# One output product in 93 places is split into two 64-row halves and issued between the halves of three U/V products

## The chip, the cores and the metric

The kernel runs on one core of one Trainium2 chip. The metric is the device time of one execution in microseconds (us). The engines named below are PE (TensorE, the matrix engine; PEld is its weight loads), DVE (VectorE), ACT (ScalarE), POOL (GpSimd) and SP (SyncE, which issues the DMAs). Each engine takes its instructions in program order.

## The reference, cut to what matters

```python
# attention through 49 agents: q, k, v are (4, 12544, 128), agents (4, 49, 128)
agent_v = softmax(scale * agents @ k.T) @ v          # per batch, 49 x 128
x = softmax(scale * q @ agents.T) @ agent_v          # per batch, 12544 x 128
x = x.reshape(50176, 128)
# feed-forward with a maximum of three: w1, w2, w3 are 128 x 768, w_out 768 x 128
h = maximum(maximum(x @ w1, x @ w2), x @ w3)
out = h @ w_out
```

## The kernel before, in words

**What is computed where.** Each batch first folds agent_v with the weights into a table G with 49 rows, stored twice, at partitions 0 to 48 and 64 to 112. Its columns hold agent_v times (w3-w1) (768 columns), times (w2-w1) (768), and a linear part through w1 and w_out. The maximum of three is taken as w1 + max(relu(w3-w1), w2-w1), where the w1 part goes through the linear table. For the fifth hidden block (f = 4) the second difference is added onto the relu in place and a second relu follows; there the columns are w3-w2 and w2-w1.

**Stages.** The 50176 rows of q are worked on in 49 stages, s = 0 to 48. Stage s has 1024 rows, or 8 tiles of 128 rows; the exponentials of its scores, e.s (128 x 512), hold the odd tiles' 49 agents at partitions 64 to 112 and the even tiles' at 0 to 48. Six hidden blocks f of 128 columns are computed in each stage. The operations on the path of the change, with their names in the order string and their lines in the kernel before, are these:

- u.s.f and v.s.f (PE, L558): one U or V product. It is a pair of matmuls of 49 rows each, one on the upper and one on the lower half of the array's rows, each with 512 columns. They write the two banks of one PSUM buffer of class UV. There are 3 UV buffers.
- a.s.f (ACT, L571, or L565 for f = 4): relu of u.s.f. For f other than 4 it writes a bf16 tile and so frees the UV buffer; for f = 4 it writes in place, and v.s.4 accumulates onto it.
- x.s.f (DVE, L574: maximum of v.s.f with the relu; or ACT, L568 for f = 4): writes r.s.f, the hidden block in bf16, and frees the UV buffer.
- li.s.o (PE, L582) and p.s.o.f (PE, L592): for each half o of the stage's tiles, an output tile o.s.o (128 x 512, PSUM class OM, 2 buffers) takes the linear part and then six output products. One output product p.s.o.f is four matmuls of 128 rows by 128 columns, with r.s.f as the weights and w_out as the moving operand.
- ov.s.o (DVE, L599): scales the output tile by the reciprocals of the softmax sums, once all six p.s.o.f are in.

Beside these run sc and ex (scores and exponentials), su and re (softmax sums and their reciprocals on DVE, L550), qt and qe (transposes of q, evacuated by DVE, L527), the work on k and v of the next batch (ks, kv on PE, kx on ACT, va on DVE, L465), casts on POOL, and loads and stores on SP.

**Array tilings.** The class Plan marks three kinds of PE work: ROW (two halves of the array's rows work beside each other: u and v), FULL (the whole array: p, li, su, ks, kv, transposes) and COL (two halves of its columns: sc).

**What sets the order.** The order of all operations is written out by hand in the string ORDER, one word an operation; the number behind a slash is the buffer that its new tile takes. Emit.run walks through the words, makes the new tiles and issues the operation. A new tile in a buffer makes its first writer wait until the last reader of the buffer's former tile is done. Since each engine runs its own words in order, ORDER fixes five queues.

Of the kernel before, what the change touches and what calls it, by code (L numbers as in the profile page):

```python
# [611 lines left out]
def kernel(  # L612
# [17 lines left out]
    plan = Plan()  # L630
    graph(plan, em)
    order, given = [], {}
    for word in ORDER.split():
        name, _, slots = word.partition("/")
        order.append(name)
        if slots:
            given[name] = [int(x) for x in slots.split(",")]
# [22 lines left out]
p.0.1.0 u.2.3/0 ov.0.1 u.2.4/2 a.2.3/2 v.1.0/1 ks1.1/1 x.1.0/4 li.1.0/0 p.1.0.2 a.2.4 su.2 p.1.0.3 p.1.0.5 re.2/0 v.2.5/0 kx1.1/0  # L660
u.2.1/1 v.2.4 x.2.5/6 a.2.1/0 p.1.0.4 kv1.1 p.1.0.1 p.1.0.0 x.2.4/3 va1.1 v.2.1/0 ov.1.0/1 v.2.3/1 vc1.2/0 sc.3/1 x.2.3/1 u.2.2/2
ex.3/0 li.1.1/0 p.1.1.4 kc1.3/1 a.2.2/1 p.1.1.2 x.2.1/0 ks1.2/1 p.1.1.0 v.2.2/1 kx1.2/3 kc1.4/2 u.2.0/2 kt1.3/0 p.1.1.5 x.2.2/4
a.2.0/2 kv1.2 su.3 p.1.1.1 p.1.1.3 kl1.5/11 u.3.5/0 re.3/2 va1.2 v.2.0/1 ov.1.1 vl1.5/5 a.3.5/1 u.3.1/2 li.2.0/1 ql.6/3 x.2.0/7
p.2.0.3 p.2.0.4 kl1.6/6 a.3.1/0 qt.4/0 ql.7/10 u.3.4/0 qe.4/0 kt1.4/2 u.3.3/1 a.3.4 v.3.5/2 p.2.0.5 x.3.5/2 p.2.0.2 p.2.0.0
a.3.3/2 vc1.3/0 p.2.0.1 kl2.1/12 sc.4/0 ov.2.0/2 v.3.4 ex.4/1 v.3.3/2 ea1.0/0 v.3.1/1 x.3.4/5 x.3.3/8 li.2.1/1 vl2.0/7 p.2.1.5
ks1.3/0 su.4 p.2.1.4 kx1.3/1 x.3.1/6 u.3.2/0 u.4.5/2 a.3.2/2 kv1.3 p.2.1.3 kc1.5/1 p.2.1.0 va1.3 re.4/1 v.3.2/1 a.4.5/0 u.3.0/0
x.3.2/7 li.3.0/0 qc.5/0 p.3.0.5 kt1.5/0 a.3.0/1 p.2.1.2 p.2.1.1 u.4.3/2 ov.2.1 ea1.1 v.3.0/1 a.4.3/2 u.4.4/0 vl1.7/9 x.3.0/0
p.3.0.3 ql.9/11 qt.5/1 vc1.5/0 a.4.4 p.3.0.4 u.4.1/2 qe.5/0 v.4.5/1 qc.6/0 a.4.1/1 v.4.4 x.4.5/4 p.3.0.2 p.3.0.1 x.4.4/1 p.3.0.0
ea1.2 sc.5/1 ov.3.0/3 v.4.1/1 u.4.2/2 ex.5/2 kc1.6/0 v.4.3/0 x.4.1/3 li.3.1/0 a.4.2/0 p.3.1.4 p.3.1.5 vc1.4/2 ks1.4/1 kt1.6/1
x.4.3/5 u.5.5/1 kx1.4/3 v.4.2/2 p.3.1.0 a.5.5/1 qc.7/1 su.5 kv1.4 x.4.2/0 kl1.7/2 u.4.0/0 vl1.6/6 p.3.1.2 a.4.0/2 p.3.1.1 kc1.8/2  # L670
kl1.9/10 p.3.1.3 re.5/0 va1.4 u.5.3/2 ov.3.1 v.4.0/1 a.5.3/0 u.5.4/0 ql.8/3 x.4.0/8 qt.6/1 li.4.0/0 a.5.4 p.4.0.3 u.5.1/2 qe.6/0
v.5.5/1 a.5.1/2 vl1.8/8 p.4.0.5 x.5.5/6 p.4.0.0 p.4.0.1 sc.6/1 v.5.1/2 ex.6/0 v.5.4 u.5.2/1 x.5.1/7 ql.10/5 p.4.0.2 a.5.2/1
p.4.0.4 li.4.1/1 p.4.1.5 ov.4.0/4 v.5.2/2 x.5.4/2 qc.9/0 vl2.3/4 u.6.5/1 x.5.2/4 p.4.1.4 ks1.5/0 a.6.5/2 p.4.1.3 vc1.7/2 p.4.1.0
v.5.3/0 u.6.4/2 kx1.5/0 kl1.10/0 u.5.0/1 x.5.3/8 a.6.4 p.4.1.1 kv1.5 su.6 p.4.1.2 a.5.0/1 re.6/2 va1.5 v.5.0/0 ov.4.1 v.6.4
ql.14/11 qt.7/0 x.6.4/0 x.5.0/3 li.5.0/1 p.5.0.5 p.5.0.3 u.6.3/1 vc1.6/0 vl1.10/9 v.6.5/2 qe.7/0 a.6.3/1 u.6.1/0 p.5.0.1 x.6.5/5
# [6 lines left out]
u.8.5/1 st.1 va1.7 u.8.4/2 ov.6.1 a.8.5/1 v.7.0/0 li.7.0/1 x.7.0/5 p.7.0.3 p.7.0.1 a.8.4 qt.9/0 ql.13/8 u.8.1/1 qe.9/0 v.8.5/0
a.8.1/2 v.8.4 x.8.5/4 p.7.0.5 p.7.0.2 vl2.1/6 p.7.0.0 x.8.4/2 p.7.0.4 sc.9/0 ov.7.0/0 v.8.3/0 ex.9/0 v.8.1/1 u.8.2/2 x.8.3/1
ks1.8/1 a.8.2/1 li.7.1/0 su.9 p.7.1.4 p.7.1.2 x.8.1/9 p.7.1.3 kx1.8/3 kc2.0/2 u.9.5/2 v.8.2/0 a.9.5/0 p.7.1.0 re.9/2 x.8.2/6
u.8.0/1 kv1.8 vc1.9/2 a.8.0/2 p.7.1.1 p.7.1.5 va1.8 u.9.3/2 ov.7.1 v.8.0/0 ea1.6 a.9.3/1 u.9.4/1 x.8.0/8 qt.10/1 li.8.0/0 a.9.4
ea1.7 p.8.0.2 p.8.0.5 qe.10/0 u.9.1/2 v.9.5/0 kc1.10/1 a.9.1/2 v.9.4 x.9.5/0 p.8.0.4 p.8.0.0 p.8.0.1 qc.14/2 x.9.4/5 kt1.10/0
p.8.0.3 sc.10/1 ov.8.0/1 v.9.1/0 ex.10/1 u.9.2/2 kc2.1/0 v.9.3/1 x.9.1/3 kl2.5/11 a.9.2/0 ks1.9/0 li.8.1/1 st.2 p.8.1.3 vc2.3/3
p.8.1.0 st.5 kx1.9/0 x.9.3/7 u.9.0/2 kt2.0/2 v.9.2/0 a.9.0/2 su.10 p.8.1.5 qc.11/0 p.8.1.1 x.9.2/8 kv1.9 p.8.1.2 ql.12/4 p.8.1.4
ea1.8 u.10.5/2 ql.15/9 v.9.0/1 re.10/1 va1.9 a.10.5/0 u.10.3/0 ql.18/12 ov.8.1 qc.13/1 qt.11/0 kl2.4/0 x.9.0/2 li.9.0/1 a.10.3/1
# [174 lines left out]
```

## Time and profile before

| what | value |
|---|---|
| median of 2 runs | 449.47 us (448.12 to 450.82) |
| the profiled execution, device time | 448.96 us |
| its span, first to last instruction | 447.1 us |
| granted TensorE clock, mean | 0.988 |
| PE, DVE, ACT, POOL busy | 421.8, 392.1, 393.6, 169.5 us |
| matmuls, and weight loads | 5260 each |

How to read it: a busy time is the time in which at least one instruction of the engine was under way. Matmuls overlap in the pipeline and their ends are modelled, so a busy PE may still have short gaps between streams. PEld overlaps PE. An idle time is put down to whatever released the engine, and gaps of 0.15 us or less are not listed as waits. Everything between the stages runs beside everything else, so a share of the span says little until one asks what waits for what.

### The profile page before, as it was taken

Reading aid. Unit: us, or ns where it says so; the run is one execution under the profiler, and the core shown is the slowest. Engines: PE = TensorE matmul, PEld = TensorE weight load, DVE = VectorE, ACT = ScalarE, POOL = GpSimd, SP = SyncE. Lnnn points to the kernel's source line nnn. Section 1 sums busy time; section 2 is a strip of 40 time slices with the busy share of each in tenths; the row PEclk is TensorE's granted clock in tenths of the full one; section 3 lists DMA queues with packets and bytes.
Section 4 is the critical chain, followed back from the end, with each engine's and each line's share of the span. In section 5 each row is a group of like instructions: output and inputs, shape, how many; then the busy total and the mean of one; then the engine's idle time right before and its main releaser. Section 6 shows DMA issues by size and latency. Waiting matters only on the chain.

```text
span 447.1 us, 12853 instructions
## 1 busy us (share of the span) xinstructions
PE 421.8 (94%) x5260; PEld 270.8 (61%) x5260; DVE 392.1 (88%) x496; ACT 393.6 (88%) x461; POOL 169.5 (38%) x176
## 2 busy tenths in 40 slices
...
DMA packets 97045, 121.98 MB, mean 273 GB/s; under 512 B 70423, under 2 KB 73179, under 8 KB 96987
## 3 DMA queue, kind: packets, MB, share of 16 engines
...
q10 hardware_dynamic: 203, 0.10, 0.1%
...
## 4 chain that ended last, share of the span: by engine, by line
PE 83%; DMA 8%; DVE 3%; issue 2%; POOL 2%; ACT 1%; SPq 1%; DVEq 0%; POOLq 0%
PE UV L558 35%; PE OM L592 31%; PE OM L582 6%; DMA LD<-in_v_dram 4%; PE OM L533 3%; DVE R L574 2%; PE OM L523 2%; DMA LD<-in_k_dram 2%; PE OM L376 2%; PE OM L359 2%; DMA LD<-in_q_dram 1%; PE OM L545 1%; SPq L325 1%; DVE OS L599 1%; POOL QB L517 1%
## 5 line engine op out<-in xcount | busy, mean ns | idle before, releaser
L574 DVE TENSOR_TENSOR R<-UV,AS 128x1024 bf16<-128x1024 f32 x245 | 293.4, 1219 | 17.8 <-PE UV L558 12.9
L571 ACT ACTIVATE AS<-UV 128x1024 bf16<-128x1024 f32 x245 | 246.3, 1024 | 17.8 <-PE UV L558 13.5
L558 PE MATMUL UV<-EQ,G 49*128 49x512 bf16 (+1 forms) x1248 | 181.7, 371 | 0.9
L592 PE MATMUL OM<-wo_bf,R 128*128 128x128 bf16 x2352 | 180.4, 220 | 0.0
L592 PEld LDWEIGHTS <-R 128*128 128x128 bf16 x2352 | 139.8, 98 | 43.4 <-issue 41.1
L558 PEld LDWEIGHTS <-G 49*128 49x128 bf16 x1248 | 61.5, 94 | 61.8 <-issue 21.7
L517 POOL CAST QB<-LD 128x1024 bf16<-128x1024 f32 x49 | 51.1, 1048 | 98.4 <-DMA LD<-in_q_dram 50.3
L335 POOL CAST KB<-LD 128x1152 bf16<-128x1152 f32 (+2 forms) x45 | 49.7, 1116 | 60.4 <-DMA LD<-in_k_dram 42.8
L599 DVE TENSOR_TENSOR OS<-OM,RC 128x512 f32<-128x512 f32 x98 | 67.1, 684 | 3.6 <-PE OM L592 2.5
L335 POOL CAST VB<-LD 128x1152 bf16<-128x1152 f32 (+1 forms) x33 | 37.3, 1137 | 47.7 <-DMA LD<-in_v_dram 14.7
L565 ACT ACTIVATE UV<-UV 128x1024 f32<-128x1024 f32 x49 | 49.8, 1017 | 2.5 <-PE UV L558 1.2
L568 ACT ACTIVATE R<-UV 128x1024 bf16<-128x1024 f32 x49 | 50.1, 1023 | 1.7 <-PE UV L558 1.2
L582 PE MATMUL OM<-G,EQ 128*128 128x256 bf16 x196 | 37.9, 276 | 0.0
L539 ACT ACTIVATE EQ<-OM 128x512 bf16<-128x512 f32 x49 | 29.5, 602 | 0.9 <-PE OM L533 0.6
L474 POOL TENSOR_TENSOR EA<-EA,EK 128x441 f32<-128x441 f32 x27 | 27.6, 1023 | 4.8 <-ACT EK L365 4.1
L347 DVE COPY KT<-UV 128x1152 bf16<-128x1152 bf16 (+1 forms) x12 | 8.2, 700 | 17.3 <-PE UV L342 17.3
L582 PEld LDWEIGHTS <-EQ 128*128 128x128 bf16 x196 | 12.6, 97 | 15.6 <-issue 14.2
L533 PE MATMUL OM<-QT,agT 128*64 128x512 bf16 (+1 forms) x104 | 20.4, 398 | 0.2 <-DMA QT<-QB 0.2
L365 ACT ACTIVATE EK<-OM 128x441 bf16<-128x441 f32 (+1 forms) x33 | 17.8, 540 | 2.9 <-POOL EA L474 1.6
L376 PE MATMUL OM<-EK,VB 128*128 128x49 bf16 x392 | 17.3, 186 | 2.7 <-ACT VB L333 1.4
L359 PEld LDWEIGHTS <-KT 128*128 128x128 bf16 x392 | 14.6, 98 | 7.5 <-issue 4.5
L376 PEld LDWEIGHTS <-VB 128*128 128x128 bf16 x392 | 14.3, 97 | 7.9 <-issue 5.0
...
## 6 DMA issues: line engine op xcount, KB each, us to landing
...
KT<-KB SPq DMA_TRANSPOSE x33, 7.0
```

What stands on the lines that cost most here:

```text
L335: (self.nc.gpsimd if eng == POOL else self.nc.vector).tensor_copy(out=out, in_=src)
L376: self.nc.tensor.matmul(out, vb[:, j, :], e[:, j * A:(j + 1) * A], start=False, stop=True, skip_group_check=True)
L517: return lambda: self.nc.gpsimd.tensor_copy(out=self.t[f"qb.{s}"], in_=self.t[f"q.{s}"][:, :GT, :])
L533: self.nc.tensor.matmul(self.t[f"qs.{s}"][h * H:(h + 1) * H, jj * P:(jj + pairs) * P], self.agT[:, b, :], self.t[f"qT.{s}"][:, 2 * jj + h: ...
L558: self.nc.tensor.matmul(t[:, h, jj * P:(jj + pairs) * P], self.t[f"G{b}"][h * H:h * H + A, c + f * P:c + (f + 1) * P], self.t[f"e.{s}"][h ...
L565: return lambda: self.nc.scalar.activation(self.t[f"u.{s}.{f}"], self.t[f"u.{s}.{f}"], AF.Relu)
L568: return lambda: self.nc.scalar.activation(self.t[f"r.{s}.{f}"], self.t[f"u.{s}.{f}"], AF.Relu)
L571: return lambda: self.nc.scalar.activation(self.t[f"a.{s}.{f}"], self.t[f"u.{s}.{f}"], AF.Relu)
L574: return lambda: self.nc.vector.tensor_tensor(out=self.t[f"r.{s}.{f}"], in0=self.t[f"v.{s}.{f}"], in1=self.t[f"a.{s}.{f}"], op=ALU.max)
L582: self.nc.tensor.matmul(self.t[f"o.{s}.{o}"][:, i * 2 * C:(i + 1) * 2 * C], self.t[f"e.{s}"][:, jj * P:(jj + 1) * P], self.t[f"G{of[jj]}"] ...
L592: self.nc.tensor.matmul(self.t[f"o.{s}.{o}"][:, c:c + C], self.t[f"r.{s}.{f}"][:, h, jj * P:(jj + 1) * P], self.wo_bf[:, f, :], start=Fals ...
L599: self.nc.vector.tensor_tensor(out=self.t[f"os.{s}"][:, j:j + 4, :], in0=self.t[f"o.{s}.{o}"].rearrange("p (j c) -> p j c", c=C), in1=self ...
```

## The change

In 93 places, four words of ORDER become one word joined by plus signs: three U/V products and one output product. Emit.run hands such a word to the new function beside. It splits the output product's 128 contraction rows in two halves of 64, so that four matmuls become eight, and issues one half of them behind the first half of the first U/V product and the other half behind the last U/V product. Behind the first half stands a further matmul of one column (named fence), into the buffer that the third U/V product is going to use. Which half of the rows comes first alternates for each output tile. Buffer numbers are those of before. On ACT, DVE, POOL and SP the order of the operations is the same as before; on PE 295 of 1536 places in the order hold another operation.

```diff
-    def run(self, plan, order, given):
+    def run(self, plan, order, given, joint):
         self.place = plan.places(order, given)
+        done = set(x for k, v in joint.items() for x in v if x != k)
         for name in order:
-            o = plan.ops[plan.index[name]]
-            for t in o["new"]:
+            if name in done:
+                continue
+            group = joint.get(name, [name])
+            if len(group) > 1:
+                self.beside(plan, group[:-1], group[-1])
+                continue
+            for t in plan.ops[plan.index[name]]["new"]:
                 self.new(plan.tiles[t], t)
-            o["fn"]()
+            plan.ops[plan.index[name]]["fn"]()
+
+    def beside(self, plan, hidden, product):
+
+        ps, o, pf = (int(x) for x in product.split(".")[1:])
+
+        def one(name, h):
+            kind, s, f = name.split(".")
+            s, f = int(s), int(f)
+            start = kind == "u" or f != FI
+            t = self.t[f"u.{s}.{f}" if kind == "u" or not start else f"v.{s}.{f}"]
+            c = (C31 if kind == "u" else C21) + f * P
+            return self.nc.tensor.matmul(t[:, h, :], self.t[f"G{s // WHOLE}"][h * H:h * H + A, c:c + P], self.t[f"e.{s}"][h * H:h * H + A, :],
+                                  start=start, stop=True, skip_group_check=True)
+
+        def rows(k):
+            for i in range(4):
+                h, jj = i % 2, 2 * o + i // 2
+                self.nc.tensor.matmul(self.t[f"o.{ps}.{o}"][:, i * C:(i + 1) * C],
+                                             self.t[f"r.{ps}.{pf}"][k:k + H, h, jj * P:(jj + 1) * P], self.wo_bf[k:k + H, pf, :],
+                                             start=False, stop=True, skip_group_check=True)
+
+        for t in plan.ops[plan.index[hidden[0]]]["new"] + plan.ops[plan.index[hidden[1]]]["new"]:
+            self.new(plan.tiles[t], t)
+        a = self.side.get((ps, o), 1)
+        self.side[ps, o] = 1 - a
+        one(hidden[0], 1 - a)
+        rows(a * H)
+        fence = self.new("UV", plan.ops[plan.index[hidden[2]]]["use"][0])
+        self.nc.tensor.matmul(fence[:, 0, :1], self.wo_bf[a * H:a * H + H, pf, :], self.wo_bf[a * H:a * H + H, pf, :1], start=True, stop=True,
+                              skip_group_check=True)
+        one(hidden[0], a)
+        one(hidden[1], 1 - a)
+        for t in plan.ops[plan.index[hidden[2]]]["new"]:
+            self.new(plan.tiles[t], t)
+        one(hidden[1], a)
+        one(hidden[2], 1 - a)
+        one(hidden[2], a)
+        rows((1 - a) * H)
...
-p.0.0.5 kt1.2/0 x.0.2/6 ks1.0/1 p.0.0.0 u.1.2/2 kx1.0/1 v.1.3/0 vc1.0/0 a.1.2/0 kl1.3/5 p.0.0.4 x.1.3/7 u.2.5/1 vl1.2/3 p.0.0.2
+p.0.0.5 kt1.2/0 x.0.2/6 ks1.0/1 p.0.0.0 kx1.0/1 vc1.0/0 kl1.3/5 u.1.2/2+v.1.3/0+u.2.5/1+p.0.0.4 a.1.2/0 x.1.3/7 vl1.2/3 p.0.0.2
...
+ov.31.1 a.33.3/2 vc3.10/2 qt.34/0 x.32.0/9 li.32.0/1 a.33.4 p.32.0.5 qc.37/0 qe.34/1 u.33.1/0+v.33.4+v.33.5/2+p.32.0.3 a.33.1/1
...
```

In 67 of the places the output product stood directly ahead of the three U/V products on PE before, in 18 it stood between them, and in 8 directly behind them. Where one of the three is a v.s.4, which accumulates onto an old tile, it never stands third; in 26 places it stands second.

More of the change, by code (lines that the diff above doesn't have):

```diff
@@ L632 @@
     order, given = [], {}
+    joint = {}
     for word in ORDER.split():
[L634 to L637, printed above, removed]
+        names = []
+        for part in word.split("+"):
+            name, _, slots = part.partition("/")
+            names.append(name)
+            if slots:
+                given[name] = [int(x) for x in slots.split(",")]
+        order += names
+        if len(names) > 1:
+            joint[names[0]] = names
     assert sorted(order) == sorted(plan.index)
     with tc.manual_schedule():
-        em.run(plan, order, given)
+        em.side = {}
+        em.run(plan, order, given, joint)
 ORDER = """
@@ L660 @@
[L660 to L675, printed above, removed]
+kl1.8/8 vc1.1/0 a.1.4 qe.3/0 qc.4/0 u.1.0/2+v.1.4+v.1.1/0+p.0.1.4 a.1.0/0 x.1.1/2 p.0.1.1 vl1.3/4 p.0.1.5 p.0.1.3 x.1.4/0 p.0.1.2
@@ new lines @@
+u.2.3/0+u.2.4/2+v.1.0/1+p.0.1.0 ov.0.1 a.2.3/2 ks1.1/1 x.1.0/4 li.1.0/0 p.1.0.2 a.2.4 su.2 p.1.0.3 re.2/0 kx1.1/0
+v.2.5/0+v.2.4+u.2.1/1+p.1.0.5 x.2.5/6 a.2.1/0 p.1.0.4 kv1.1 p.1.0.1 p.1.0.0 x.2.4/3 va1.1 v.2.1/0 ov.1.0/1 v.2.3/1 vc1.2/0 sc.3/1
+x.2.3/1 u.2.2/2 ex.3/0 li.1.1/0 p.1.1.4 kc1.3/1 a.2.2/1 p.1.1.2 x.2.1/0 ks1.2/1 p.1.1.0 v.2.2/1 kx1.2/3 kc1.4/2 u.2.0/2 kt1.3/0
+p.1.1.5 x.2.2/4 a.2.0/2 kv1.2 su.3 p.1.1.1 kl1.5/11 re.3/2 va1.2 vl1.5/5 u.3.5/0+v.2.0/1+u.3.1/2+p.1.1.3 ov.1.1 a.3.5/1 li.2.0/1
@@ L682 @@
[L682 to L689, printed above, removed]
@@ new lines @@
+v.7.2/1 a.7.0/2 p.6.1.3 x.7.2/3 p.6.1.4 ql.11/9 ks1.7/1 v.7.1/2 kx1.7/0 u.8.3/0 x.7.1/0 p.6.1.1 a.8.3/0 kv1.7 su.8 p.6.1.0 re.8/0
+st.1 va1.7 u.8.5/1+u.8.4/2+v.7.0/0+p.6.1.5 ov.6.1 a.8.5/1 li.7.0/1 x.7.0/5 p.7.0.3 p.7.0.1 a.8.4 qt.9/0 ql.13/8 qe.9/0
+u.8.1/1+v.8.4+v.8.5/0+p.7.0.5 a.8.1/2 x.8.5/4 p.7.0.2 vl2.1/6 p.7.0.0 x.8.4/2 p.7.0.4 sc.9/0 ov.7.0/0 v.8.3/0 ex.9/0 v.8.1/1
+u.8.2/2 x.8.3/1 ks1.8/1 a.8.2/1 li.7.1/0 su.9 p.7.1.4 p.7.1.2 x.8.1/9 p.7.1.3 kx1.8/3 kc2.0/2 re.9/2
+u.9.5/2+v.8.2/0+u.8.0/1+p.7.1.0 a.9.5/0 x.8.2/6 kv1.8 vc1.9/2 a.8.0/2 p.7.1.1 va1.8 ea1.6 u.9.3/2+v.8.0/0+u.9.4/1+p.7.1.5 ov.7.1
@@ new lines @@
+a.12.5/2 li.11.0/0 u.12.3/1+v.11.0/2+u.12.4/0+p.11.0.4 a.12.3/1 st.3 x.11.0/9 p.11.0.5 p.10.1.5 p.10.1.4 a.12.4 ov.10.1 st.4
+u.12.1/1+v.12.4+v.12.5/2+p.11.0.1 a.12.1/0 x.12.5/4 p.11.0.3 p.11.0.0 p.11.0.2 x.12.4/6 sc.13/1 ov.11.0/7 v.12.1/1 v.12.3/2
+ex.13/1 kt2.4/2 u.12.2/0 x.12.1/3 li.11.1/0 a.12.2/2 p.11.1.5 ks2.1/1 su.13 p.11.1.2 x.12.3/5 kx2.1/3 ql.17/0 v.12.2/1 u.12.0/0
+kv2.1 a.12.0/0 p.11.1.4 x.12.2/2 u.13.3/2 p.11.1.3 a.13.3/1 p.11.1.0 re.13/1 va2.1 u.13.5/1+u.13.4/0+v.12.0/2+p.11.1.1 ov.11.1
@@ new lines @@
+qc.21/2 x.19.5/3 kt2.9/0 p.18.0.0 p.18.0.4 p.18.0.5 x.19.4/5 p.18.0.1 kc2.10/2 sc.20/0 ov.18.0/1 qd.21/2 v.19.1/2 ex.20/2 v.19.3/1
+u.19.2/0 x.19.1/0 ea2.5 li.18.1/1 a.19.2/0 p.18.1.4 ks2.8/0 ql.24/5 p.18.1.1 x.19.3/6 st.14 u.20.5/2 kx2.8/0 v.19.2/0 vl3.5/4
+a.20.5/1 p.18.1.2 kv2.8 st.13 x.19.2/1 u.19.0/1 kt2.10/1 p.18.1.5 a.19.0/2 p.18.1.3 va2.8 kl3.2/8
+u.20.3/2+v.19.0/0+u.20.4/1+p.18.1.0 ov.18.1 a.20.3/0 x.19.0/7 su.20 li.19.0/1 p.19.0.2 kc3.0/1 st.9 p.19.0.3 a.20.4 re.20/2
+vc3.1/0 u.20.1/2+v.20.4+v.20.5/0+p.19.0.1 a.20.1/2 x.20.5/4 p.19.0.5 kt3.0/2 p.19.0.4 p.19.0.0 x.20.4/9 vc2.10/2 sc.21/0 ov.19.0/6
@@ new lines @@
+v.21.3/1 kc3.2/2 vl3.4/10 ex.22/1 v.21.1/0 u.21.2/2 x.21.3/3 ks2.10/0 a.21.2/1 li.20.1/1 fo2/0 p.20.1.2 vl3.6/11 p.20.1.5 x.21.1/1
+v.21.2/1 kx2.10/2 u.22.5/2 p.20.1.1 a.22.5/0 kv2.10 x.21.2/5 u.21.0/0 kl3.3/8 to2 a.21.0/2 su.22 va2.10 re.22/1 nr2/0,2
+u.22.3/2+v.21.0/1+u.22.4/0+p.20.1.0 a.22.3/1 x.21.0/7 st.16 p.20.1.4 li.21.0/0 p.21.0.2 a.22.4 p.20.1.3 ov.20.1
+u.22.1/1+v.22.4+v.22.5/2+p.21.0.3 a.22.1/2 x.22.5/8 p.21.0.0 kc3.4/1 st.15 p.21.0.5 p.21.0.1 x.22.4/9 p.21.0.4 sc.23/1 ov.21.0/5
+qc.24/2 v.22.1/2 kt3.1/1 ex.23/2 u.22.2/1 v.22.3/0 x.22.1/4 a.22.2/0 li.21.1/0 vc3.0/2 p.21.1.4 p.21.1.2 vl3.3/5 p.21.1.5 x.22.3/0
@@ new lines @@
+x.27.2/9 u.28.5/1 a.27.0/2 p.26.1.5 li.27.0/0 p.27.0.4 ov.26.1 v.27.0/2 a.28.5/0 u.28.4/0 x.27.0/0 p.27.0.3 p.27.0.5 a.28.4
+v.28.5/1 sc.29/1 x.28.5/6 u.28.1/2 ex.29/2 p.27.0.2 p.27.0.1 a.28.1/2 p.27.0.0 v.28.4 ov.27.0/6 v.28.1/1 x.28.4/7 li.27.1/1
+x.28.1/1 p.27.1.2 ks3.5/0 kx3.5/3 v.28.3/2+u.28.2/0+u.29.5/1+p.27.1.5 x.28.3/5 a.28.2/2 p.27.1.4 kc3.6/2 kv3.5 p.27.1.0 su.29
+a.29.5/0 v.28.2/0 re.29/0 va3.5 u.28.0/2 kc3.8/1 kt3.6/0 x.28.2/0 li.28.0/0 a.28.0/1 p.27.1.3 p.28.0.3 ea3.3 vl3.9/1
+u.29.3/1+v.28.0/0+u.29.4/2+p.27.1.1 ov.27.1 a.29.3/2 x.28.0/2 qc.32/0 a.29.4 p.28.0.2 qt.30/1 qe.30/0
@@ new lines @@
+u.29.1/1+v.29.4+v.29.5/0+p.28.0.4 a.29.1/1 x.29.5/3 p.28.0.0 p.28.0.5 p.28.0.1 ov.28.0/2 x.29.4/8 sc.30/1 ex.30/0 v.29.1/0
+x.29.1/9 ql.38/4 v.29.3/1 x.29.3/4 u.29.2/2 a.29.2/0 li.28.1/0 p.28.1.0 ks3.6/1 p.28.1.1 su.30 kx3.6/2 u.30.5/0 a.30.5/1 v.29.2/2
+p.28.1.5 kl3.10/9 kc3.7/2 ql.39/8 kt3.7/1 re.30/1 x.29.2/6 p.28.1.2 vc3.7/3 u.29.0/1 a.29.0/2 p.28.1.3 kv3.6 va3.6
+u.30.4/0+v.29.0/2+u.30.3/1+p.28.1.4 ov.28.1 a.30.4 a.30.3/0 x.29.0/7 ql.33/10 qd.32/0 ql.34/5 qc.33/2 qc.34/0 kt3.8/0 st.26
+li.29.0/1 p.29.0.1 p.29.0.5 v.30.4 x.30.4/5 sc.31/0 ql.37/7 v.30.5/2 x.30.5/0 u.30.1/1 a.30.1/2 p.29.0.4 p.29.0.0 p.29.0.3 ex.31/1
@@ new lines @@
+v.30.1/0+u.30.2/2+v.30.3/1+p.29.0.2 ov.29.0/0 x.30.1/1 a.30.2/1 x.30.3/2 li.29.1/1 ks3.7/0 kx3.7/1 p.29.1.2 p.29.1.4 st.21 st.24
+qd.33/1 kt3.9/1 p.29.1.0 u.31.5/0 a.31.5/2 v.30.2/2 x.30.2/7 p.29.1.3 p.29.1.1 u.30.0/1 a.30.0/0 p.29.1.5 kv3.7 ov.29.1 su.31
+re.31/2 u.31.3/0 a.31.3/1 vc3.8/3 vl3.10/10 v.30.0/2 u.31.4/1 a.31.4 x.30.0/3 li.30.0/1 p.30.0.4 p.30.0.5 va3.7 ea3.4 ea3.5
+u.31.1/0+v.31.4+v.31.5/2+p.30.0.1 a.31.1/0 x.31.5/9 x.31.4/4 p.30.0.3 p.30.0.0 p.30.0.2 ov.30.0/3 sc.32/0 ex.32/2 v.31.3/2
@@ new lines @@
+u.31.2/0 v.31.1/1 x.31.3/8 ks3.8/1 a.31.2/2 li.30.1/0 ql.35/0 p.30.1.1 vc3.9/2 p.30.1.3 x.31.1/6 ql.43/5 v.31.2/2 kx3.8/3 u.32.5/0
+p.30.1.4 a.32.5/1 qc.36/1 p.30.1.5 x.31.2/5 u.31.0/1 kv3.8 a.31.0/0 p.30.1.2 ea3.6 qd.36/0 va3.8
+u.32.3/0+v.31.0/2+u.32.4/1+p.30.1.0 ov.30.1 a.32.3/2 kc3.10/1 x.31.0/3 su.32 li.31.0/0 st.22 p.31.0.5 p.31.0.3 a.32.4 ea3.7
+kt3.10/0 re.32/1 ea3.8 u.32.1/0+v.32.4+v.32.5/2+p.31.0.2 a.32.1/0 x.32.5/7 p.31.0.0 p.31.0.4 x.32.4/0 p.31.0.1 sc.33/1 ov.31.0/7
+v.32.1/0 ex.33/0 u.32.2/2 v.32.2/1 x.32.1/2 a.32.2/1 li.31.1/1 ks3.9/0 p.31.1.2 p.31.1.1 su.33 x.32.2/5 u.33.5/0 kx3.9/3 v.32.3/2
@@ new lines @@
+p.32.1.3 ql.40/4 x.33.2/9 u.33.0/0 ql.41/0 su.34 p.32.1.4 a.33.0/1 to3 qd.37/1 qc.43/1 va3.10 nr3/0,3
+u.34.4/2+v.33.0/1+u.34.3/0+p.32.1.1 a.34.4 re.34/2 x.33.0/0 p.32.1.2 li.33.0/0 a.34.3/0 p.33.0.5 ov.32.1
+v.34.4+v.34.5/1+u.34.1/0+p.33.0.2 x.34.4/5 x.34.5/2 p.33.0.1 p.33.0.0 p.33.0.3 a.34.1/1 p.33.0.4 sc.35/1 ov.33.0/1 v.34.3/1
+qd.38/2 ex.35/2 u.34.2/2 v.34.1/0 x.34.3/3 a.34.2/2 li.33.1/0 p.33.1.4 p.33.1.2 st.32 p.33.1.0 x.34.1/4 u.35.5/1 st.30 u.34.0/2
+a.35.5/0 ql.48/5 p.33.1.5 su.35/1 p.33.1.1 re.35/1 p.33.1.3 a.34.0/1 v.34.2/0 ov.33.1 gpl3/1 gpa3/1 x.34.2/6 gvl3 sc.36/0 gpc3/2
@@ new lines @@
+x.37.4/8 sc.38/1 ov.36.0/0 v.37.1/1 qd.39/2 v.37.3/0 ex.38/1 u.37.2/2 x.37.1/0 li.36.1/0 a.37.2/1 p.36.1.3 p.36.1.4 li.37.0/1
+x.37.3/9 p.36.1.1 u.37.0/2+v.37.2/1+u.38.2/0+p.36.1.0 a.37.0/2 x.37.2/2 p.36.1.2 a.38.2/0 p.36.1.5 ov.36.1
+v.37.0/2+u.38.0/1+v.38.2/0+p.37.0.5 qc.41/0 x.37.0/7 a.38.0/1 sc.39/0 p.37.0.2 qd.42/2 p.37.0.1 p.37.0.4 ex.39/0 x.38.2/4 u.38.1/2
+v.38.0/1 a.38.1/2 p.37.0.0 st.28 li.37.1/0 x.38.0/5 p.37.1.1 ql.47/0 ql.46/8 u.39.2/0+v.38.1/2+u.39.0/1+p.37.1.2 a.39.2/0 x.38.1/0
+p.37.1.4 a.39.0/1 u.38.4/0+v.39.2/2+u.38.5/1+p.37.0.3 ov.37.0/3 a.38.4 x.39.2/8 p.37.1.0 p.37.1.5 a.38.5/2 p.37.1.3 v.38.4 ov.37.1
@@ new lines @@
+v.39.3/1+u.41.0/2+u.40.4/0+p.39.0.2 a.41.0/1 x.39.3/3 p.39.0.5 p.39.0.1 su.40/1 p.39.0.4 re.40/0 v.41.2/2 x.41.2/9 u.40.5/1
+p.39.0.3 p.39.0.0 ov.39.0/8 a.40.4 v.40.4 sc.42/1 a.40.5/2 v.40.5/1 x.40.5/10 x.40.4/11 u.41.1/2 a.41.1/0 li.39.1/0 v.41.0/0
+x.41.0/12 p.39.1.1 p.39.1.0 ex.42/0 u.40.3/1 a.40.3/2 v.41.1/2 x.41.1/7 p.39.1.3 p.39.1.4 p.39.1.2
+u.42.0/0+v.40.3/1+u.42.2/2+p.39.1.5 a.42.0/1 x.40.3/8 ov.39.1 a.42.2/0 li.40.0/1 p.40.0.1 u.41.4/0+v.42.2/1+u.41.5/2+p.40.0.4
+a.41.4 x.42.2/1 a.41.5/2 p.40.0.2 p.40.0.0 su.41/0 re.41/2 p.40.0.3 v.41.4+u.42.1/1+v.41.5/2+p.40.0.5 ov.40.0/7 x.41.4/5 a.42.1/0
@@ new lines @@
+x.41.5/3 sc.43/1 ex.43/3 li.40.1/0 p.40.1.0 v.42.0/0+u.41.3/2+v.42.1/1+p.40.1.3 x.42.0/4 a.41.3/2 x.42.1/8 p.40.1.2 p.40.1.4
+p.40.1.1 su.42/1 re.42/1 qc.48/1 u.43.2/0+v.41.3/2+u.43.0/1+p.40.1.5 a.43.2/1 x.41.3/0 ov.40.1 a.43.0/0 li.41.0/1 p.41.0.1
+u.42.4/0+v.43.2/2+u.42.5/1+p.41.0.5 a.42.4 x.43.2/10 a.42.5/2 p.41.0.3 p.41.0.4 p.41.0.0 p.41.0.2 ov.41.0/6 v.42.4 x.42.4/11
+v.42.5/2 sc.44/0 u.43.1/1 a.43.1/1 x.42.5/6 li.41.1/1 v.43.0/0 x.43.0/2 p.41.1.2 p.41.1.5 ex.44/1 st.38 qd.47/2 qc.45/0 u.42.3/2
@@ new lines @@
+a.42.3/2 v.43.1/1 p.41.1.4 x.43.1/3 qd.46/0 li.42.0/0 p.42.0.1 st.35 qd.45/1 st.40 st.36 u.44.2/0+v.42.3/2+u.44.0/1+p.41.1.3
+a.44.2/0 x.42.3/5 a.44.0/1 p.41.1.1 p.41.1.0 ov.41.1 u.43.4/0+v.44.2/2+u.43.5/1+p.42.0.5 a.43.4 st.41 x.44.2/12 p.42.0.4 p.42.0.0
+st.39 p.42.0.3 a.43.5/2 p.42.0.2 v.43.4 ov.42.0/7 v.43.5/2 x.43.4/7 su.43/1 u.44.1/1 re.43/2 x.43.5/0 li.42.1/0 p.42.1.5 a.44.1/0
+v.44.0/0 sc.45/1 x.44.0/6 u.43.3/2 ex.45/0 v.44.1/1 p.42.1.2 a.43.3/2 p.42.1.4 li.43.0/1 x.44.1/1 p.43.0.2
+u.45.0/0+v.43.3/2+u.45.2/1+p.43.0.1 a.45.0/1 x.43.3/11 p.42.1.3 a.45.2/0 p.42.1.1 u.44.4/0+v.45.2/2+u.44.5/1+p.42.1.0 ov.42.1
@@ new lines @@
+sc.47/1 ov.44.0/6 v.46.0/2 u.46.1/1 ex.47/2 v.45.5/0 x.46.0/11 li.45.0/0 a.46.1/0 li.44.1/1 p.45.0.0 p.45.0.4 x.45.5/9 u.45.3/2
+v.46.1/1 a.45.3/1 p.44.1.5 p.44.1.2 p.44.1.3 x.46.1/5 u.47.0/0+v.45.3/2+u.47.2/1+p.44.1.1 a.47.0/2 x.45.3/2 p.44.1.4 a.47.2/0
+u.46.4/0+v.47.2/2+u.46.5/1+p.44.1.0 ov.44.1 a.46.4 x.47.2/6 su.46/1 p.45.0.2 p.45.0.3 a.46.5/1 p.45.0.5 re.46/1
+v.46.4+v.46.5/2+u.47.1/1+p.45.0.1 ov.45.0/3 x.46.4/8 x.46.5/1 li.45.1/1 p.45.1.1 p.45.1.3 a.47.1/0 v.47.0/0 sc.48/0 x.47.0/2
+u.46.3/2 ex.48/0 v.47.1/1 p.45.1.2 a.46.3/1 p.45.1.4 x.47.1/7 li.46.0/0 p.45.1.5 p.45.1.0 u.47.5/2 u.48.2/0 ov.45.1 a.47.5/2
```

246 lines of the change are left out of this document (100 added, 146 removed).

## The prediction

> **What bounds the kernel now.** I read the page first: its span, its busy times, and the costliest groups.
>
> ```profile
> span 447.1 us, 12853 instructions
> PE 421.8 (94%) x5260; PEld 270.8 (61%) x5260; DVE 392.1 (88%) x496; ACT 393.6 (88%) x461; POOL 169.5 (38%) x176
> ...
> L574 DVE TENSOR_TENSOR R<-UV,AS 128x1024 bf16<-128x1024 f32 x245 | 293.4, 1219 | 17.8 <-PE UV L558 12.9
> L571 ACT ACTIVATE AS<-UV 128x1024 bf16<-128x1024 f32 x245 | 246.3, 1024 | 17.8 <-PE UV L558 13.5
> ...
> L599 DVE TENSOR_TENSOR OS<-OM,RC 128x512 f32<-128x512 f32 x98 | 67.1, 684 | 3.6 <-PE OM L592 2.5
> ```
>
> All three compute engines are close to full. The reader should see the means (a maximum on DVE 1.22 us, a relu on ACT 1.02, an output scaling on DVE 0.68) and how little DVE and ACT wait for PE today. Leaving out the start and the end, the busy times from 60 to 440 us are:
>
> ```profile
> 60.00:440.00 380.00, 377.74 (x4727) 242.29 (x4726) 360.32 (x437) 356.91 (x413) 144.47 (x147) 1.00 0.91 260
> ```
>
> The columns are PE, PEld, DVE, ACT, POOL, granted clock, DMA share and GB/s. In 380 us DVE is idle for 380 - 360.3 = 19.7, ACT for 23.1, and the clock is full. PE shows no idle time, but its ends are modelled, so I went to the starts of its matmuls. Between 60 and 435 us (375 us) the columns streamed fill 305 us, the changes between array tilings another 51, and 20 are left, nearly all short waits for a UV buffer. The prices come from the timeline:
>
> ```profile
> 203.09 0.85 PE L558 MATMUL UV<-EQ,G 49*128 49x512 bf16 x6
> ...
> 203.87 1.07 PE L592 MATMUL OM<-wo_bf,R 128*128 128x128 bf16 x16
> ...
> 204.87 0.41 PE L533 MATMUL OM<-QT,agT 128*64 128x512 bf16 x2
> ```
>
> Three U/V pairs take 0.213 to 0.22 each; sixteen output matmuls start (1.07 - 0.22)/15 = 0.056 apart. The sixteen end streaming at 203.87 + 16 x 0.056 = 204.77, and the next tiling starts at 204.87: a change costs 0.10 us.
>
> Last, one of the 93 places, u.20.3, v.19.0, u.20.4 with p.18.1.0, in the timelines of PE, ACT and DVE:
>
> ```profile
> 208.44 0.84 PE L592 MATMUL OM<-wo_bf,R 128*128 128x128 bf16 x12
> 209.22 0.82 PE L558 MATMUL UV<-EQ,G 49*128 49x512 bf16 x6
> ...
> 207.41 3.26 ACT L571 ACTIVATE AS<-UV 128x1024 bf16<-128x1024 f32 x3
> ...
> 208.03 1.23 DVE L574 TENSOR_TENSOR R<-UV,AS 128x1024 bf16<-128x1024 f32 x1
> 209.17 0.20 DVE L465 TENSOR_TENSOR VA<-OM,VA 128x49 f32<-128x49 f32 x1
> 209.32 0.69 DVE L599 TENSOR_TENSOR OS<-OM,RC 128x512 f32<-128x512 f32 x1
> 209.93 1.23 DVE L574 TENSOR_TENSOR R<-UV,AS 128x1024 bf16<-128x1024 f32 x1
> ```
>
> The second relu of ACT's three (a.19.0) ends at 209.57 and frees the buffer of u.20.4, whose pair, the third, starts at 209.66: each buffer is freed just before PE needs it. The third relu (a.20.3) reads the first pair from 209.65, 0.43 after that pair's start. DVE goes from one operation to the next without a hole, since p.18.1.0, the last four matmuls at 208.44, is in before ov.18.1 starts at 209.32. So three buffers, two readers and one writer run in close step; a delay of one is not hidden.
>
> **The change, part by part.** *Array changes.* In the order string, PE changes its tiling 583 times before and 546 times after. 37 fewer at 0.10 us: -3.5 us. Only the 18 places where the output product stood alone between two of the three U/V products give these; in the 67 where it stood ahead of them, the run of output products just gets shorter.
>
> *Streaming.* A half array of 64 rows still streams every column: a product's four matmuls become two times four of 128 columns. One half of the rows runs first half of U/V, second, third, then four matmuls; the other four matmuls, fence, then three halves. Is 0.056 kept for 64-row matmuls with new weights each? The nearest row is the last stage, whose pairs are 49 rows by 128 columns:
>
> ```profile
> 435.22 0.84 PE L558 MATMUL UV<-EQ,G 49*128 49x128 bf16 x24
> ```
>
> Twelve pairs start (0.84 - 0.22)/11 = 0.056 apart, so yes. A fence of one column costs between nothing and 0.056; the 49-column products of L376 start 0.025 apart, the nearest row, and I take that. A group then takes 0.224 + 0.025 + 2 x 0.213 + 0.224 = 0.90 us; before, three pairs and one product took 3 x 0.213 + 0.224 = 0.86. That is +0.04 x 93 = +3.7 us. The 465 added matmuls and weight loads are inside it. Array changes and streaming together: +0.2 us.
>
> *The wait that the fence brings.* The fence writes the third product's buffer, so it waits for that buffer's reader, and behind it on PE stand the second half of the first product and all that follows. Before, this wait came two pairs later, with a product ahead of the three. In the place above the group can start at 208.90 (where p.18.1.0 stood) and reaches the fence at 209.12; the buffer is free at 209.57, and held matmuls start 0.05 after the release: 209.62, a stall of 0.50 us. Then the first product's second half starts at 209.64 and its relu at 209.64 + 0.43 = 210.07 instead of 209.65. The second half of p.18.1.0 starts at 210.07, its last matmul 0.17 later, and ov.18.1 0.26 after that (0.22 for a matmul, 0.04 to the reader): 210.50 instead of 209.32. DVE runs in order, so x.19.0 behind it is as late. PE ends the group at 210.30 instead of 209.88.
>
> I worked the same steps through all 93 places with the starts and ends of before. 91 fences stall, by 0.50 us in the median. PE is late by 0.43 in the median and 35.4 us in sum; ACT's next operation by 0.41, sum 39.5. DVE's next operation is the output scaling in 32 places: late by 1.18, sum 37.5. In 61 it is a maximum: late by 0.47, sum 30.2. DVE's sum is 67.7 us.
>
> These are not to be added over engines: they are one delay seen three times. They can't be hidden by the other engines' work either, as each engine runs in order. DVE has the largest, and can make good at most its idle time, 19.7 us. So I take 67.7 - 19.7 = 48.0. The ends: at each place the least of the three delays, 28.8 in sum, and the greatest, 71.7.
>
> *Moves.* The other queues keep their order, so nothing is moved past anything on SP or POOL; loads and casts only get more time. In 26 places a v.s.4 stands second and waits for the relu in its own buffer; that is in the sums.
>
> **Sum.** The profiled execution took 448.96 us, 1.9 beyond its span and 0.5 under the median of the runs, 449.47. 448.96 + 48.0 = 497 us. The 0.2 us above is not added again: the delays were worked with the new group lengths and array changes.
>
> **The rivals.** *Not slower.* The fence costs nothing if the third buffer is free 0.17 us after the group's start. Then only +0.2 is left: 449 us. For it: a PE that comes later to each place finds buffers free. Against it: PE must come 0.50 later than ACT and DVE at each place, while the wait makes ACT and DVE late by as much or more; 2 places of 93 have it so today. Faster by over 2% would need 9 us less of PE's work, and the changes saved are 3.5.
>
> *PE's delay alone.* If the output scaling's lateness is absorbed, since a late DVE meets PE's next products already done, the sum is PE's: 449 + 35 = 484 us. For it: PE is the fullest engine. Against: the next group's fence often waits for the very maximum that DVE then runs late.
>
> *The short matmuls don't run beside the long one.* If a matmul started after another could not end before it, the halves of the output product would be held: its first matmul would end with the 512-column half that it runs beside, at 0.213 instead of 0.056. The first half hides this in the stall; the second adds 0.157 at the group's end, 93 x 0.157 = 14.6 us: 512 us. No pair of unequal length stands in this trace. The Trainium skill says just this ("TensorE: Matmul & The Clock Gate", section "The mechanism"): matmuls start and end in strict program order, also over different tiles of the array. By that rule the sum would be 512 and not 497, and no row here shows it yet.
>
> **How the numbers follow.** 0.55 for the forecast (DVE in order, 497), 0.22 for PE alone (484), 0.10 for the held halves (512), 0.08 for not slower (449), and 0.05 for more than the upper end. The range goes from the least to the greatest delays, 448.96 + 28.8 = 477.7 and 448.96 + 71.7 = 520.7: 478 to 521, which holds all but the last two. A measurement of this kernel tells some 2% from no change. Slower by over 2%: 0.90; within 2%: 0.08; faster: 0.02.
>
> **What would show it.** The fence's line gets waits of about 0.5 us for ACT or DVE in most places; DVE's wait for PE before the output scaling rises from 2.5 us to 30 or more; the busy time of DVE stays near 392 us while its share falls to 79%. Eight 64-row matmuls 0.056 apart beside a 512-column half would confirm the streaming; 0.21 or more would speak for the held halves. I am wrong if fences find their buffers free, or if DVE's idle time grows by well under 30 us.

## The result, and the profile after

The changed kernel takes 510.85 us (median of 2 runs, 510.06 to 511.64) against 449.47: 1.137 times the time before, 95% interval 1.120 to 1.153. The forecast was 497 us with a range of 478 to 521. The profiled execution of the changed kernel took 511.64 us, with a span of 509.7, 62.6 more than before.

The page of the changed kernel, busy times and the groups that answer to those shown of before (L617 is the maximum on DVE, L614 the relu on ACT, L642 the output scaling, L344 the fence):

```profile
span 509.7 us, 13747 instructions
PE 439.1 (86%) x5725; PEld 290.4 (57%) x5725; DVE 392.8 (77%) x496; ACT 397.9 (78%) x461; POOL 169.6 (33%) x176
...
L617 DVE TENSOR_TENSOR R<-UV,AS 128x1024 bf16<-128x1024 f32 x245 | 293.8, 1219 | 42.6 <-PE UV L327 30.8
L614 ACT ACTIVATE AS<-UV 128x1024 bf16<-128x1024 f32 x245 | 246.2, 1023 | 60.2 <-PE UV L327 47.0
...
L642 DVE TENSOR_TENSOR OS<-OM,RC 128x512 f32<-128x512 f32 x98 | 67.1, 685 | 40.8 <-PE OM L333 33.8
...
L344 PE MATMUL UV<-wo_bf 64*128 64x1 bf16 x93 | 15.0, 162 | 21.9 <-ACT AS L614 12.2
```

DVE does the same work in the same time per instruction (1219 ns, 392.8 us in all). What grew is the idle time in front of it: before maxima from 17.8 to 42.6 us, before output scalings from 3.6 to 40.8. Together that is +62.0 us, and the span grew by 62.6. L333, the halves of the output product, is now what the scaling waits for, and L327, the U/V products in the groups, what maxima and relus wait for.

The same place as in the prediction (u.20.3, v.19.0, u.20.4, p.18.1.0), in the changed kernel's timeline of PE:

```profile
232.41 0.39 PE L327 MATMUL UV<-EQ,G 49*128 49x512 bf16 x1
232.41 0.39 PE L333 MATMUL OM<-wo_bf,R 64*128 64x128 bf16 x4
233.03 0.16 PE L344 MATMUL UV<-wo_bf 64*128 64x1 bf16 x1 [0.23 <-ACT AS L614]
233.04 0.60 PE L327 MATMUL UV<-EQ,G 49*128 49x512 bf16 x4
...
233.55 0.33 PE L333 MATMUL OM<-wo_bf,R 64*128 64x128 bf16 x3
...
234.71 0.38 PE L625 MATMUL OM<-G,EQ 128*128 128x256 bf16 x2 [0.65 <-DVE OS L642]
```

and of ACT and of DVE:

```profile
233.47 1.02 ACT L614 ACTIVATE AS<-UV 128x1024 bf16<-128x1024 f32 x1 [0.49 <-PE UV L327]
```

```profile
233.96 0.69 DVE L642 TENSOR_TENSOR OS<-OM,RC 128x512 f32<-128x512 f32 x1 [1.18 <-PE OM L333]
234.57 1.22 DVE L617 TENSOR_TENSOR R<-UV,AS 128x1024 bf16<-128x1024 f32 x1
```

Four short matmuls start between 232.41 and 232.59 beside the first half of u.20.3. Then PE stands until 233.03, when ACT has freed the third buffer. The line at 233.04 holds four U/V matmuls: the first of them is the first half of v.19.0, on the other 64 rows of the array, and the second half of u.20.3 starts at 233.06, behind the fence on the same 64 rows. ACT waits 0.49 us for it, and DVE waits 1.18 us for the second half of p.18.1.0, the 1.18 us of the prediction. The last PE line shows a consequence that the prediction did not name: the output tiles have 2 buffers, so a late scaling also holds the linear part of a later tile, here for 0.65 us.

### The profile page after: what moved, and what is told of

The parts are those of the page before. It is cut to its first block, busy times and chain, and to the rows that moved or that the text cites. A ratio compares the mean times of both kernels' runs of the same rounds, so it can differ in the third digit from the quotient of the medians.

```text
span 509.7 us, 13747 instructions
## 1 busy us (share of the span) xinstructions
PE 439.1 (86%) x5725; PEld 290.4 (57%) x5725; DVE 392.8 (77%) x496; ACT 397.9 (78%) x461; POOL 169.6 (33%) x176
## 4 chain that ended last, share of the span: by engine, by line
PE 49%; DVE 20%; ACT 11%; issue 9%; DMA 8%; POOL 1%; SPq 1%; DVEq 0%; ACTq 0%; POOLq 0%
DVE R L617 16%; PE OM L635 13%; PE UV L601 11%; PE UV L327 10%; ACT AS L614 8%; DMA LD<-in_v_dram 5%; DVE OS L642 5%; PE OM L333 3%; PE OM L625 3%; PE UV L344 2%; DMA LD<-in_k_dram 2%; PE OM L576 2%; DMA LD<-in_q_dram 1%; ACT R L611 1%; PE OM L402 1%
## 5 line engine op out<-in xcount | busy, mean ns | idle before, releaser
L617 DVE TENSOR_TENSOR R<-UV,AS 128x1024 bf16<-128x1024 f32 x245 | 293.8, 1219 | 42.6 <-PE UV L327 30.8
L614 ACT ACTIVATE AS<-UV 128x1024 bf16<-128x1024 f32 x245 | 246.2, 1023 | 60.2 <-PE UV L327 47.0
L635 PE MATMUL OM<-wo_bf,R 128*128 128x128 bf16 x1980 | 155.6, 221 | 0.0
L635 PEld LDWEIGHTS <-R 128*128 128x128 bf16 x1980 | 119.2, 98 | 31.0 <-issue 22.9
L327 PE MATMUL UV<-EQ,G 49*128 49x512 bf16 x558 | 112.6, 381 | 3.2 <-DVE R L617 1.2
L601 PE MATMUL UV<-EQ,G 49*128 49x512 bf16 (+1 forms) x690 | 99.1, 361 | 7.5 <-DVE R L617 4.9
L642 DVE TENSOR_TENSOR OS<-OM,RC 128x512 f32<-128x512 f32 x98 | 67.1, 685 | 40.8 <-PE OM L333 33.8
L333 PE MATMUL OM<-wo_bf,R 64*128 64x128 bf16 x744 | 73.1, 219 | 0.4 <-DVE R L617 0.3
L333 PEld LDWEIGHTS <-R 64*128 64x128 bf16 x744 | 49.1, 95 | 25.1 <-issue 2.3
L327 PEld LDWEIGHTS <-G 49*128 49x128 bf16 x558 | 29.1, 93 | 42.9 <-issue 31.4
L344 PE MATMUL UV<-wo_bf 64*128 64x1 bf16 x93 | 15.0, 162 | 21.9 <-ACT AS L614 12.2
L582 ACT ACTIVATE EQ<-OM 128x512 bf16<-128x512 f32 x49 | 29.5, 603 | 2.3 <-PE OM L576 2.2
L625 PEld LDWEIGHTS <-EQ 128*128 128x128 bf16 x196 | 13.7, 97 | 24.5 <-issue 22.7
L390 DVE COPY KT<-UV 128x1152 bf16<-128x1152 bf16 (+1 forms) x12 | 8.2, 699 | 17.8 <-PE UV L385 17.8
```

The costliest lines, as they stand in the source:

```text
L327: return self.nc.tensor.matmul(t[:, h, :], self.t[f"G{s // WHOLE}"][h * H:h * H + A, c:c + P], self.t[f"e.{s}"][h * H:h * H + A, :], start ...
L333: self.nc.tensor.matmul(self.t[f"o.{ps}.{o}"][:, i * C:(i + 1) * C], self.t[f"r.{ps}.{pf}"][k:k + H, h, jj * P:(jj + 1) * P], self.wo_bf[k ...
L601: self.nc.tensor.matmul(t[:, h, jj * P:(jj + pairs) * P], self.t[f"G{b}"][h * H:h * H + A, c + f * P:c + (f + 1) * P], self.t[f"e.{s}"][h ...
L614: return lambda: self.nc.scalar.activation(self.t[f"a.{s}.{f}"], self.t[f"u.{s}.{f}"], AF.Relu)
L617: return lambda: self.nc.vector.tensor_tensor(out=self.t[f"r.{s}.{f}"], in0=self.t[f"v.{s}.{f}"], in1=self.t[f"a.{s}.{f}"], op=ALU.max)
L625: self.nc.tensor.matmul(self.t[f"o.{s}.{o}"][:, i * 2 * C:(i + 1) * 2 * C], self.t[f"e.{s}"][:, jj * P:(jj + 1) * P], self.t[f"G{of[jj]}"] ...
```

## The experiments

Theory A is the prediction's: the fence waits for the third buffer, the output product ends behind the three U/V products, and DVE, in order, loses what it waits at these places. B: the 64-row halves themselves cost the time. C: the fence's wait alone is the cost. D: only the late output scaling counts.

**The fence into the second product's buffer.** A kernel with the halves and no fence wasn't tried: both halves of the output product write the same PSUM bank from different rows of the array, and the fence, on which the third product waits, is meant to keep them in order; no run here shows whether it is needed. In 67 places the fence was put into the second product's buffer instead.

```diff
-        for t in plan.ops[plan.index[hidden[0]]]["new"] + plan.ops[plan.index[hidden[1]]]["new"]:
+        second = plan.ops[plan.index[hidden[1]]]["new"]
+        for t in plan.ops[plan.index[hidden[0]]]["new"]:
             self.new(plan.tiles[t], t)
...
-        fence = self.new("UV", plan.ops[plan.index[hidden[2]]]["use"][0])
+        fence = self.new("UV", (second or plan.ops[plan.index[hidden[2]]]["use"])[0])
...
         one(hidden[0], a)
+        for t in second:
+            self.new(plan.tiles[t], t)
         one(hidden[1], 1 - a)
```

> The fence stays, but in the 67 places where the second product takes a new buffer it writes that buffer and not the third's; in the other 26 (a v.s.4 stands second) it stays where it was. Everything else is the changed kernel. Theory A (DVE's queue is made late by the fence's wait and by the output product that now ends behind the three): worked through the 93 places with the buffer times of the kernel before, the stalls at the fence fall from 40.6 to 16.1 us and DVE's delays from 67.7 to 46.8 us (31.2 before output scalings, 15.6 before maxima). The changed kernel kept 62 of its 67.7, so I expect 449 + 43 = 492 us. Theory B (the 64-row halves themselves cost the time, whichever buffer the fence writes): 508 to 512 us. Theory C (the fence's wait alone is the cost, the late output product costs nothing): stalls 16 of 41, so 449 + 62 x 16/41 = 474 us.

Measured: 496.41 us, ratio to before 1.110 (1.105 to 1.115). Its groups, the maximum on DVE and the output scaling:

```profile
L620 DVE TENSOR_TENSOR R<-UV,AS 128x1024 bf16<-128x1024 f32 x245 | 293.7, 1219 | 31.2 <-PE UV L327 19.8 <-PE UV L604 5.0 <-PE OM L333 3.7
L645 DVE TENSOR_TENSOR OS<-OM,RC 128x512 f32<-128x512 f32 x98 | 67.2, 686 | 36.8 <-PE OM L333 32.8 <-PE OM L638 2.1 <-DMA LD<-in_v_dram 1.0
```

Idle time before maxima falls from 42.6 to 31.2, before scalings only from 40.8 to 36.8. Theory A gave 492. B falls as the whole cause: every half is still there and 14 us are gone. C falls too: the kernel is far from 474, because the scaling stays late.

**The whole product behind the three, no halves, no fence.**

```diff
-        one(hidden[0], 1 - a)
-        rows(a * H)
...
-        one(hidden[2], a)
-        rows((1 - a) * H)
+        for name in hidden:
+            whole(name)
+        whole(product)
```

Here whole(name) makes the operation's new tiles and issues it as Emit.run does.

> No halves and no fence: in each of the 93 places the three U/V products are issued as before, and the whole output product (128 rows, four matmuls) right behind them. Theory A: only the lateness of the output product is left, with a little from the new order of the U/V products; by the places DVE is late by 33.9 us before output scalings and 9.9 before maxima, so some 449 + 40 = 489 us, with DVE's wait before output scalings near the 40.8 us of the changed kernel. Theory C (the fence's wait alone): 449 to 455 us. Theory B (the halves): also 449 to 455.

Measured: 482.72 us, ratio 1.077 (1.075 to 1.080). Its waits and groups:

```profile
DVE OS L633 <- PE OM L626: 36.1, 41, 1.2
```

```profile
L608 DVE TENSOR_TENSOR R<-UV,AS 128x1024 bf16<-128x1024 f32 x245 | 293.0, 1218 | 17.9 <-PE UV L592 11.7 <-PE OM L626 4.1 <-ACT UV L599 0.2
L633 DVE TENSOR_TENSOR OS<-OM,RC 128x512 f32<-128x512 f32 x98 | 67.3, 687 | 36.8 <-PE OM L626 36.1
```

Issuing the product behind the three, with the U/V products in their new order, costs 35 us over the 447.81 of the kernel before, measured beside it: idle time before scalings is 36.8 us, before maxima 17.9, as in the kernel before. Theory A is near, 6 us too high: of the 9.9 us that it put before maxima, nothing came.

**The whole product ahead, no halves, no fence.** As above, with whole(product) ahead of the loop.

> No halves and no fence: the whole output product is issued ahead of the three U/V products in each of the 93 places. In 67 of them it stood there before; in 26 it moves ahead, which joins two runs and saves about 36 array changes of 0.10 us. Theory A: near the kernel before, 449 us, between 446 (the array changes saved) and 460 (16 us of maxima late in places where the output product moves ahead of U/V products or a v.s.4 stands second). If the order of the U/V products itself were the cause, it would be near 510.

Measured: 459.44 us, ratio 1.026 (1.023 to 1.028), at the upper end of what was expected. So 50 of the 62 us are in the halves' late place and the fence, and 11.6 in what this kernel keeps of the new order.

**The fence alone.** The whole product ahead, then the fence into the third buffer, then the three.

```diff
...
+        a = 1
+        whole(product)
         fence = self.new("UV", plan.ops[plan.index[hidden[2]]]["use"][0])
         self.nc.tensor.matmul(fence[:, 0, :1], self.wo_bf[a * H:a * H + H, pf, :], self.wo_bf[a * H:a * H + H, pf, :1], start=True, stop=True,
                               skip_group_check=True)
...
+        for name in hidden:
+            whole(name)
```

> The fence alone: the whole output product is issued ahead as in the run above, then the fence into the third product's buffer, then the three U/V products as they were. The output product is early, the wait for the third buffer stands in front of the first product. Theory A: by the places DVE is late by 30.6 us before maxima and 10.4 behind output scalings, so 449 + 38 = 487 us; DVE's wait before output scalings stays near the 3.6 us of the kernel before. Theory D (only the late output scaling counts, U/V products that come late are absorbed in idle time): 449 to 460 us.

Measured: 491.50 us, ratio 1.097 (1.094 to 1.101). Its waits:

```profile
DVE R L612 <- PE UV L596: 56.4, 98, 1.2
PE UV L345 <- ACT AS L609: 22.2, 42, 1.0
PE UV L345 <- DVE R L612: 11.7, 29, 0.9
DVE OS L637 <- PE OM L630: 2.1, 5, 0.6
```

The fence (L345) waits for the readers of the third buffer, 33.9 us in the listed waits, and DVE then waits 56.4 us for U/V products, while the scalings are on time. D falls: late U/V products are not absorbed. Against the run without the fence it costs 32 us.

**The change at one kind of place only.** The 93 places fall into 61 in which DVE's next operation is a maximum and 32 in which it is the output scaling. At the places undone, the whole product goes ahead.

```diff
             if len(group) > 1:
-                self.beside(plan, group[:-1], group[-1])
-                continue
+                if group[-1] not in SCALED:
+                    self.beside(plan, group[:-1], group[-1])
+                    continue
+                first, second, third, product = group
+                for x in (product, first, third, second) if product in SWAPPED else (product, first, second, third):
+                    for t in plan.ops[plan.index[x]]["new"]:
+                        self.new(plan.tiles[t], t)
+                    plan.ops[plan.index[x]]["fn"]()
+                continue
```

The diff is that of the run that keeps the 61; the other has "in SCALED". SCALED lists the output products of the 32 places; SWAPPED those of the 23 in which the change had put a v.s.4 ahead of another product.

> The change is kept in the 61 places where DVE's next operation is a maximum, and undone in the 32 where it is the output scaling (there the whole output product goes ahead of the three U/V products, in their former order). Theory A (DVE's queue in order): the maxima are late by 30.2 us in sum by the places of the kernel before, so some 449 + 28 = 477 us; DVE's idle time before output scalings falls back from 40.8 to under 10 us. Theory C (the fence's wait alone, the same at both kinds of place, 0.50 us in the median): 61 of 93 parts of the loss, 448 + 62 x 61/93 = 489 us.

> The other way about: the change is kept in the 32 places with the output scaling next on DVE, and undone in the 61 others. Theory A: the scalings are late by 37.5 us in sum, so some 449 + 36 = 485 us, more than from twice as many places of the other kind; both losses together give the whole, 62 us, within 5. Theory C: 32 of 93 parts, 448 + 62 x 32/93 = 469 us.

Measured: 478.67 us for the 61 (ratio 1.066, 1.063 to 1.069) and 488.47 us for the 32 (1.087, 1.083 to 1.092). The output scaling of each, first with the 61, then with the 32:

```profile
L649 DVE TENSOR_TENSOR OS<-OM,RC 128x512 f32<-128x512 f32 x98 | 66.9, 682 | 2.4 <-PE OM L642 1.9
```

```profile
L649 DVE TENSOR_TENSOR OS<-OM,RC 128x512 f32<-128x512 f32 x98 | 67.2, 686 | 39.4 <-PE OM L340 36.2 <-PE OM L642 1.7 <-DMA LD<-in_v_dram 1.0
```

A third of the places makes more than half of the loss, as A says and C does not. The 32 places alone cost 36.5 us of span, of which the products moved at the other 61 can be at most 3.3 (the next run). In the prediction PE's delays come to 35.4 us over all 93 places, and ACT's to 39.5, so neither engine's own delay can be the price of 32; DVE's 37.5 us for these 32 is near it. The two losses, 30.0 and 39.8 us over the 448.72 of the kernel before, measured beside them, add to 69.7. The places undone in one run are those kept in the other, so the 4 us that the next run shows for a whole product moved ahead are in this sum once. That leaves 66 us, 4 more than the whole change lost. By the profiled spans the parts add up: 29.6 + 36.5 - 3.3 = 62.8 us against 62.6. (The profiled run of the 32 places is the fastest of its four, which took 485.36 to 490.30 us.)

**The product ahead, U/V in their former order.**

```diff
-                self.beside(plan, group[:-1], group[-1])
+                first, second, third, product = group
+                for x in (product, first, third, second) if product in SWAPPED else (product, first, second, third):
...
```

> The whole output product ahead in all 93 places, as in the run that measured 459.4 us, but in the 23 places where the change had put a v.s.4 ahead of another product, the three U/V products stand in their former order. Only the 26 moved output products then differ from the kernel before. Theory A1 (the new order of U/V made the 11.6 us): 444 to 449 us, down to 3.5 us below the kernel before for the 36 array changes saved. Theory A2 (moving the lone output products ahead of U/V products made it): still near 459 us.

Measured: 452.74 us, ratio 1.009 (1.006 to 1.012). The former order gives back about 7 of the 11.6 us, so theory A1 holds for the larger part. The other 4 us, 0.9%, stay. That is under the 2% by which kernels are told apart here, though the interval lies above 1. This kernel changes its array tiling 549 times against 583, counted in its order, and is at any rate no faster. Its maximum on DVE shows where:

```profile
L621 DVE TENSOR_TENSOR R<-UV,AS 128x1024 bf16<-128x1024 f32 x245 | 294.2, 1220 | 20.6 <-PE UV L605 16.3 <-ACT AS L618 0.2 <-issue 0.2
```

Idle time before maxima is 20.6 us against 17.8. That moving a lone product ahead of U/V products makes these late fits it, but which of the 26 moves does it was not tried. No kernel here beats the one before.

All profiles together, each against the kernel before (447.1 us span; 17.8 us idle before maxima, 3.6 before scalings). The last column is the sum over the places as the expectations gave it:

| kernel | span | idle before maxima + scalings | place sum |
|---|---|---|---|
| changed | +62.6 | +62.0 | 67.7 |
| fence in the second buffer | +46.8 | +46.6 | 46.8 |
| whole product behind | +33.7 | +33.3 | 43.8 |
| whole product ahead | +10.6 | +10.3 | 16 |
| product ahead, fence | +42.9 | +41.2 | 41.0 |
| changed at 61 places | +29.6 | +29.5 | 30.2 |
| changed at 32 places | +36.5 | +36.1 | 37.5 |
| ahead, former order | +3.3 | +2.4 | not worked out |

DVE's busy time is 391.9 to 394.2 us in every kernel, so its idle time has to grow with the span, whatever the cause. What the table adds is where: nearly all of it stands ahead of these two operations. It doesn't show that DVE alone sets the time. ACT's idle time before its relus grows as well (17.8 to 60.2 us in the changed kernel), and the chain of work that ended last runs through PE for 83% of the span before and 49% after, through DVE for 3% and 20%. That DVE's lateness counts rests on the last column, and on the 32 places above all. With nothing taken off for idle time, the place sum is within 2 us of the span's growth in four kernels, 5 too high in two and 10 in the one with the product behind.

## Why the prediction was right, and where its size was off

*Array changes and streaming, +0.2 us in sum.* Near in its parts. In the changed trace the short matmuls start 0.056 us apart beside the 512-column half, and from the fence to the end of a group it takes 0.68 us in the median (0.621 to the last start, and 0.056), where the lengths used gave 0.025 + 2 x 0.213 + 0.224 = 0.675. The two shortest groups, whose fences found the buffer free, took 0.94 us in all (0.880 to the last start, and 0.056), where 0.90 was worked out. The halves bring nothing: each half of the array streams all the columns. The saved array changes did not show as a gain either (452.74 us with 549 changes).

*The fence's wait.* Right, a little too large: 84 of the 93 fences start over 0.10 us behind the short matmul ahead of them, not 91. The time beyond 0.055 us is 34.5 us in sum and 0.39 in the median, against 40.6 and 0.50.

*DVE's delay, 37.5 us before scalings and 30.2 before maxima.* Right: the idle time rose by 37.2 and 24.8. One small term was too short: the prediction lets the scaling start 0.26 us after the last matmul starts. That holds behind a whole product (0.257 us, median of 41 waits in the run with the product behind); behind the halves it is 0.305 us (median of 29 waits), for a reason that no run here shows.

*The idle time that makes it good, -19.7 us.* This is the term that was mis-sized. The prediction took off all of DVE's idle time between 60 and 440 us and came to 48.0; the profiled span grew by 62.6, so about 5 us were made good. The step took idle time as a reserve that can be moved to where it is needed. In the trace of before, 9.2 of the 19.7 us stand directly ahead of the very operations that became late, and were already counted, since each delay was taken from start to start. The rest are waits for a buffer or a product too; they move along with everything else when DVE is late. The last is argued from the table, not shown by a run that moves one of them. The range held because its upper end was the greatest of the delays with no idle time taken off (71.7 us); the forecast itself was 14 us low.

*The rivals.* PE's delay alone (484 us) falls: with the product behind and no fence, 35 us are lost, and with the change at 32 places alone 36.5 us of span, as much as PE's delays at all 93 places. Not slower (449) falls with the waits at the fence. The held halves gave 512 us, and 510.85 was measured, but that is a coincidence: the 14 us that the forecast lacked are the idle time above. The held halves fall by the starts: of the four short matmuls, the second starts 0.066 us after the first (median of the 93 places), not 0.21, and behind the last one DVE starts 0.05 us later than behind a whole product, not 0.157. The recorded ends are modelled, so whether they end in order, as the Trainium skill says ("TensorE: Matmul & The Clock Gate", section "The mechanism"), these traces cannot tell; the starts are not held by it. That section of the Trainium skill has the starts in program order too. Here they are not in that order from one half of the rows to the other (83 of the 93 places, last section), and the measurement decides.
